# A smaller descriptor scratch for GpSimd, and seven more weight units kept in SBUF

## The chip, the cores and the metric

The kernel runs on one core of one Trainium2 chip. The metric is the device time of one execution in microseconds; a kernel's time is the median of several runs. Engines carry the names of the profile: PE (TensorE), PEld (its weight loads), DVE (VectorE), ACT (ScalarE), POOL (GpSimd), SP (SyncE).

## What is computed

The output mixes two branches of the same 2048 x 1024 input `x` by a sigmoid gate per row. Branch A is attention that runs segment by segment: 64 segments of 32 rows, each joined with 8 memory rows, and the first 8 rows of a segment's output are the next segment's memory. Branch B is a feed-forward block with 3584 hidden columns.

```python
for s in range(n_seg):                      # 64 segments, one after the other
    h = concatenate([mem, x[32*s:32*s+32]]) # 40 rows x 1024
    q, k, v = h @ Wq, h @ Wk, h @ Wv        # 32 heads of 128, each weight 1024 x 4096
    p = softmax(where(mask, q @ k.T * scale, -1e9))
    o = (p @ v) @ Wo                        # Wo: 4096 x 1024
    mem = o[:8]; outs.append(o[8:])
b = (gelu(x @ w_gate) * (x @ w_up)) @ w_down
out = g * concat(outs) + (1 - g) * b        # g = sigmoid((x * gate_w).sum(-1))
```

All tensors are bfloat16. The four weights of branch A take 32 MiB, more than the SBUF holds, and each segment needs all of them.

## The kernel before

**Order of work.** The first part, about 600 us long, is branch B in four blocks of 512 rows: `emit_H` (L449: gate and up matmuls), `down_mm` (L494), `down_out` (L510, L514: scaled copies to SBUF; L519: stores to `b_scr` in DRAM). In the same time SP copies streamed weights into one contiguous DRAM buffer, `w_scr` (`copy_wide`, L603), and POOL handles the gate values (`emit_gates`): one store of 2048 fp32 values to DRAM (L380), then 24 loads that spread them over partitions (`gload`, L385). Then come the 64 segments, strictly one after the other: memory rows of segment s are transposed and copied into `hT` at its end (L1370, L1376), and segment s+1 starts from `hT`.

**A segment.** A weight unit is 128 x 1024 (256 KiB). PE runs six projections in the order q0, k0, q1, v0, k1, v1 (`emit_P`, L958; the digit is the half of the heads), each over eight units of the contraction, and then four output groups of eight units (`emit_O`, L1121). Between them, in an order written out by hand at the end of the file, stand the transposes of q and k (`emit_T`, L1003), the scores (`emit_S`, L1038), the transposes of the probabilities (`emit_PT`, L1068) and the products with v (`emit_PV`, L1079). Each group of heads has a chain that leaves PE: scores, then DVE, ACT, DVE (L1045 to L1058, tile `pn`), `emit_PT` on PE, a DVE copy (L1073), `emit_PV` on PE, an ACT copy (L1087). Rows that a later segment takes as extra query, key and value rows are computed four segments at a time on spare matmuls (`xe`, L843, L1104) and go through DRAM: `qk_scr` (L887), `v_scr` (L860), and back as `qkst` (L715) and `vt` (L727).

**Where weights lie.** Most units stay in SBUF for all segments, in `arena`. Of each projection the units 6 and 7, and of the output groups the units 4 to 7, are streamed: `wide` lists the pairs, 19 blocks of two units (512 KiB) a segment, except that group 3 keeps its units 4 and 5. Three further units of q0 are kept in odd places. They are copied once into PSUM banks that would be idle (`KEPT`, `keep`), and put back into `vt`, `qk`, and `oT` with `rows` at the end of every segment: `back_all` (L944, L946) for unit 5, `back` (L935) for the second half of unit 4.

**The ring.** Streamed blocks go into `ring`, ten slots of one unit, so five blocks. SP issues the next load (L621) when PE has done with a block: `slot_free` counts slots, and each load waits for the matmuls that read its slots last. Loads are taken in the order of use.

**POOL's queue.** All other transfers inside the segments are issued by POOL in program order: `hT`, `xe`, `qkst`, `vt`, `bo`, the output rows (L1386) and the stores to `qk_scr` and `v_scr`. For these the descriptors lie in a scratch of SBUF, 16 KiB of each partition, that the framework sets aside at address 0.

```python
wide += [("o", o, k) for o in range(NO) for k in (4, 6) if (o, k) != (3, 4)]
...
KEPT = {("q", 0, 5, 0): [(6, 0, 0, 1024)], ("q", 0, 5, 1): [(7, 0, 0, 1024)],
        ("q", 0, 4, 1): [(3, 384, 0, 640), (5, 640, 640, 384)]}
...
emit_O(1, (1,))   # unit 4 of output group 1: a streamed block
emit_PT(2)
emit_S(3)
```

Of the kernel before, what the change touches and what calls it, by code (L numbers as in the profile page):

```python
# [5 lines left out]
BF16 = mybir.dt.bfloat16  # L6
# [122 lines left out]
def bass_gated_mix__memory_aug_recurrent_mem_tr__geglu_ffn__prompt_kernel(  # L129
# [21 lines left out]
    SEG = 32  # L151
# [16 lines left out]
    with ExitStack() as es:  # L168
# [11 lines left out]
        w_scr = nc.dram_tensor("w_scr", [19, 128, 2048], BF16)  # L180
        g_scr = nc.dram_tensor("g_scr", [S], FP32)

        def SB(shape, dt, name):
# [187 lines left out]
        def emit_gates(b):  # L371
            zs, ths = [("z", t) for t in range(4 * b, 4 * b + 4)], [("th", t) for t in range(4 * b, 4 * b + 4)]
            gv, zv = g_all[:, 4 * b:4 * b + 4], omg[:, 4 * b:4 * b + 4]
            op("act", lambda e: e.activation(gv, zv, ACTF.Tanh, scale=0.5), r=zs, w=ths)
            op("dve", lambda e: e.tensor_scalar(out=zv, in0=gv, scalar1=-0.5, scalar2=0.5,
                                                op0=ALU.mult, op1=ALU.add), r=ths, w=zs)
            op("dve", lambda e: e.tensor_scalar(out=gv, in0=gv, scalar1=0.5, scalar2=0.5,
                                                op0=ALU.mult, op1=ALU.add), r=ths, w=ths)
            if b == 3:
                op("pool", lambda e: e.dma_start(g_scr[:].rearrange("(t p) -> p t", p=128), g_all[:, :],  # L380
                                                 allow_slow_non_contiguous=True),
                   r=[("th", x) for x in range(NT)], w=[("gscr",)], dsem="gscr")

                def gload(dst, src, key):
                    op("pool", lambda e: e.dma_start(dst, src, allow_slow_non_contiguous=True),  # L385
                       r=[("gscr",), ("gz",)], w=[("gseg", key)], dsem="gseg%s" % key)

                for q in range(4):
                    gload(gseg[32 * q:32 * q + SEG, 0:NSEG - 1],
                          g_scr[EXT:EXT + (NSEG - 1) * SEG].rearrange("(s r) -> r s", r=SEG), "a%d" % q)  # L390
                    gload(gseg[32 * q:32 * q + NR, NSEG - 1:NSEG],
                          g_scr[S - SEG + EXT:S].rearrange("(s r) -> r s", s=1), "b%d" % q)
                    for u in range(GR):
                        gload(ge[32 * q + u * EXT:32 * q + (u + 1) * EXT, :],
                              g_scr[:].rearrange("(g s r) -> s r g", s=GR, r=SEG)[u, 0:EXT, :], "e%d%d" % (q, u))
# [156 lines left out]
        single = {("q", 0, 4): (half21[:, 0, :], A(21)), ("o", 3, 4): (half21[:, 1, :], A(22))}  # L552
        single[("o", 3, 5)] = (extra[:, :], A(23))

        def load_single(n):
# [4 lines left out]

        KEPT = {("q", 0, 5, 0): [(6, 0, 0, 1024)], ("q", 0, 5, 1): [(7, 0, 0, 1024)],
                ("q", 0, 4, 1): [(3, 384, 0, 640), (5, 640, 640, 384)]}
        flat_vt = vt[:, :, :].rearrange("p a b -> p (a b)")
        flat_qk = qk[:, :, :, :, :].rearrange("p a b c d -> p (a b c d)")
        flat_oT = oT[:, :, :, :].rearrange("p a b c -> p (a b c)")
        K_VT = [("vt", 0), ("vt", 1)] + [("vte", x) for x in range(2)] + [("vte", x, 0) for x in range(2)]
        K_QK = [("qk", 0), ("qk", 1), ("qke",)]
        K_OT = [("oT", 0), ("oT", 1)]
        BACK = {("q", 0, 5, 0): ([flat_vt[:, 0:512], flat_vt[:, 512:1024]], K_VT),
                ("q", 0, 5, 1): ([flat_qk[:, 0:512], flat_qk[:, 512:1024]], K_QK),  # L570
                ("q", 0, 4, 1): ([flat_oT, rows[:, :]], K_OT + [("rows",)])}

        wide = []
        for m, h in (("q", 0), ("k", 0), ("q", 1), ("v", 0), ("k", 1), ("v", 1)):
            wide += [(m, h, kc) for kc in (6, 7)]
        wide += [("o", o, k) for o in range(NO) for k in (4, 6) if (o, k) != (3, 4)]
        stream = []
        for s in range(NSEG):
            for u in wide:
                stream.append((s, u, 1 if u == ("o", 3, 5) else 2))  # L580
                if s == 0 and u == ("q", 0, 7):
                    stream += [(s, ("q", 0, 4), 1), (s, ("q", 0, 5), 2)]

        def uses(s, m, h, k):
            if m == "o":
                return 0 if k < 4 or (m, h, k) in single else (1 if (h, k) == (3, 5) else 2 * (k % 2))
            if m == "q" and h == 0 and s == 0 and k in (4, 5):
                return k - 3
            return 2 if k >= 6 else 0
# [42 lines left out]
        for b in range(4):  # L632
            mine, other = (b % 2) * 4, 4 - (b % 2) * 4
            for j in range(NJ):
# [31 lines left out]
                if b == 3 and j in (2, 6, 10, 14):  # L666
                    (load_single(("q", 0, 4)) if j == 2 else load_need(need[(4, 6, 7)[(j - 6) // 4]]))
                if b == 3 and j == 18:
                    slot_free(RING)
# [82 lines left out]
        def unit(s, m, o, k):  # L752
# [12 lines left out]
            else:  # L765
# [4 lines left out]
                if (m, h, k, j) in BACK:  # L770
                    if s > 0:
                        return BACK[(m, h, k, j)]
                    sl = slot_of[(s, (m, h, k), j if k == 5 else 0)]
                elif k >= 6:
# [27 lines left out]
        for s in range(NSEG):  # L802
# [117 lines left out]

            def back(eng, u, y):
                dst, c = BACK[u][0][y], y * 512
                if u[2] == 5:
                    pieces = [(KEPT[u][0][0], c, 0, 512)]
                elif y == 0:
                    pieces = [(3, 384, 0, 512)]
                else:
                    pieces = [(3, 896, 0, 128), (5, 640, 128, 384)]
                keys = BACK[u][1]
                if u[2] == 4:  # L930
                    keys = [("rows",)] if y else K_OT
                for bank, p0, c0, n in pieces:
                    d, sr = dst[:, c0:c0 + n], PBV[bank][:, p0:p0 + n]
                    if eng == "act":
                        op("act", lambda e, d=d, sr=sr: e.activation(d, sr, ACTF.Copy), r=[P(bank)], w=keys)  # L935
                    else:
                        op("dve", lambda e, d=d, sr=sr: e.tensor_copy(d, sr), r=[P(bank)], w=keys)

            def back_all(eng, u):
# [9 lines left out]
            def emit_P(m, h, pos, s=s):  # L949
                bank = acc(s, (m, h))  # L950
                for x in pos:
# [31 lines left out]
                    if s == 0 and (m, h) == ("q", 0):  # L983
# [3 lines left out]
                        for _ in range(1 + len(kept) % 2):  # L987
                            if kept:
                                kept.pop(0)()
                    if not (s == 0 and m == "q" and h == 0 and kc in (4, 5)):  # L990
                        slot_free(uses(s, m, h, kc))
# [365 lines left out]
            if s + 1 < NSEG:  # L1357
                op("act", lambda e, B_O=B_O: e.activation(rows[:, 0:256], PB[B_O][:, 0:256], ACTF.Copy),
                   r=[P(B_O)], w=[("rows",)])
                back("act", ("q", 0, 4, 1), 0)  # L1360
            fill(H)
# [3 lines left out]
            if s + 1 < NSEG:  # L1365
# [10 lines left out]
                op("dve", lambda e, mdst=mdst, msrc=msrc: e.tensor_copy(mdst, msrc), r=[P(B_PT)], w=[("hT",)])  # L1376
                back("act", ("q", 0, 4, 1), 1)
            flush()
            last = s == NSEG - 1
            op("dve", lambda e, s=s, B_O=B_O: e.scalar_tensor_tensor(  # L1380
                out=bo[:, :], in0=PB[B_O][:, 0:256], scalar=gseg[:, s:s + 1], in1=bo[:, :], op0=ALU.mult, op1=ALU.add),
               r=[P(B_O)] + [("gseg", "%s%d" % (k, q)) for k in "ab" for q in range(4)], w=[("bo", x) for x in range(4)])
            for put, bank in ends:
# [48 lines left out]
```

## Time and profile before

| what | value |
|---|---|
| median of 3 runs | 2458.86 us (2457.59 to 2460.99) |
| span of the profiled execution | 2450.2 us; its own time beside the span isn't listed, and the median is 8.7 us more than the span |
| instructions | 83,579 |
| read from DRAM, written | 764.52 MB, 37.22 MB |
| mean granted TensorE clock | 0.994 |

The span runs from the first to the last instruction of one execution. The page cuts it into 40 slices of about 61 us and gives the busy share of each engine in tenths. Groups of instructions are listed by line of the kernel, tile written and tile read, with the idle time of the engine before them and what ended it. "DMA ring<-w_scr" as the end of a wait means that the engine waited for the load of a streamed block.

### The profile page before, as it was taken

To read this page: it belongs to the slowest core of one execution; us is meant where nothing else is said; L and a number is where in the kernel's file an instruction comes from. 1 tells how busy PE (TensorE), PEld (TensorE's weight loads), DVE (VectorE), ACT (ScalarE), POOL (GpSimd) and SP (SyncE) were. 2 spreads that over 40 slices of the span, in tenths; PEclk is the share of its full clock that TensorE was granted. 3 is DMA by queue.
4 is the path that set the end of the run, shared out by engine and by line. 5 is a ranking of instruction groups with operands and counts; after the bars stand their busy time and mean duration, and the time that the engine had idled before them with its cause. 6 is when DMAs were issued, how large, how long until landed. Compare 5 with 4: busy or idle time off the path is not lost.

```text
span 2450.2 us, 83579 instructions
## 1 busy us (share of the span) xinstructions
PE 2198.1 (90%) x37171; PEld 1099.3 (45%) x37171; DVE 1182.3 (48%) x3451; ACT 934.6 (38%) x2212; POOL 628.7 (26%) x1122
## 2 busy tenths in 40 slices
PE   8999999999888888888888888888888888988887
PEld 4444444444444444444444444444444444444433
DVE  5626264351444444555445545444555545545444
ACT  4314132230434344444444444444444444444433
POOL 1010111200333323232323232233323232323222
PEclk9999999999999999999999999999999999999989
DMA  8726354458999999999999999999999999999998
GB/s 268 271 69 232 124 172 139 121 200 309 341 353 369 375 364 373 371 378 379 373 376 373 377 371 379 368 375 378 384 376 377 377 384 381 379 362 375 378 371 298
DMA packets 294008, 797.46 MB, mean 325 GB/s; under 512 B 48304, under 2 KB 112992, under 8 KB 292880
## 3 DMA queue, kind: packets, MB, share of 16 engines
q1 hardware_dynamic: 249380, 736.79, 80.7%
q0 software_dynamic: 43072, 54.77, 7.1%
q8 instruction: 292, 4.78, 0.8%
q10 hardware_dynamic: 1196, 0.56, 0.1%
q14 instruction: 68, 0.56, 0.1%
HBM read 764.52 MB, written 37.22 MB: 327 GB/s over the span
## 4 chain that ended last, share of the span: by engine, by line
PE 55%; DMA 30%; DVE 7%; ACT 5%; issue 2%; POOL 0%; SPq 0%; DVEq 0%
DMA ring<-w_scr 29%; PE pba L958 6%; PE pbb L958 6%; PE pbc L843 5%; PE pba L1121 3%; PE pbb L1121 3%; PE pbe L1068 2%; PE pbh L449 2%; PE pbg L449 2%; PE pbf L449 2%; PE pbe L449 2%; PE pba L449 2%; PE pbb L449 2%; PE pbc L449 2%; PE pbd L449 2%
## 5 line engine op out<-in xcount | busy, mean ns | idle before, releaser
L958 PE MATMUL pba<-arena,hT 128*32 128x512 bf16 x4416 | 357.1, 381 | 2.5 <-issue 2.3
L958 PE MATMUL pbb<-arena,hT 128*32 128x512 bf16 x4416 | 350.5, 382 | 1.5 <-issue 1.5
L1051 ACT ACTIVATE pbd<-pbd 104x160 f32<-104x160 f32 x256 | 71.9, 281 | 550.1 <-DVE pbd L1049 550.1
L727 POOL DMA_DIRECT2D vt<-v_scr x252 | 147.5, 589 | 395.3 <-PE pbf L1079 272.2
L1011 DVE COPY qk<-pbe 128x512 bf16<-128x512 bf16 x129 | 89.2, 692 | 317.4 <-PE pbe L1003 317.4
L1073 DVE COPY ptb<-pbe 80x320 bf16<-80x320 bf16 x256 | 82.1, 321 | 273.2 <-PE pbe L1068 273.2
L843 PE MATMUL pbc<-arena,xe 128*32 128x512 bf16 x2208 | 184.0, 380 | 1.3 <-issue 0.7
L1386 POOL DMA_DIRECT2D out_dram<-bo x252 | 125.5, 505 | 214.0 <-DVE bo L1380 205.1
L958 PE MATMUL pbb<-ring,hT 128*32 128x512 bf16 x1536 | 152.5, 386 | 30.9 <-DMA ring<-w_scr 28.4
L958 PE MATMUL pba<-ring,hT 128*32 128x512 bf16 x1542 | 153.2, 385 | 28.6 <-DMA ring<-w_scr 26.3
L958 PEld LDWEIGHTS pba<-arena,hT 128*32 128x32 bf16 x4416 | 115.9, 97 | 98.7 <-issue 6.6
L958 PEld LDWEIGHTS pbb<-arena,hT 128*32 128x32 bf16 x4416 | 115.9, 97 | 86.5 <-issue 6.1
L1058 DVE TENSOR_TENSOR pn<-pbd,rr 104x256 bf16<-104x256 f32 (+1 forms) x512 | 141.9, 318 | 8.7
L964 ACT ACTIVATE rows<-pba 128x512 bf16<-128x512 f32 x128 | 76.4, 597 | 156.0 <-PE pba L958 156.0
L887 POOL DMA_DIRECT2D qk_scr<-rowsx x60 | 47.4, 790 | 327.4 <-DVE rowsx L884 327.4
L1052 DVE TENSOR_REDUCE rs<-pbd 104x4 f32<-104x160 f32 x256 | 83.0, 324 | 88.9 <-ACT pbd L1051 88.9
L1087 ACT ACTIVATE oT<-pbf 128x256 bf16<-128x256 f32 x256 | 97.5, 381 | 74.1 <-PE pbf L1079 73.3
L1121 PE MATMUL pba<-ring,oT 128*32 128x256 bf16 x1792 | 108.6, 278 | 17.1 <-DMA ring<-w_scr 16.4
L1121 PE MATMUL pba<-arena,oT 128*32 128x256 bf16 x2176 | 119.4, 280 | 3.6 <-ACT oT L1087 1.8
L1068 PE MATMUL pbe<-ident,pn 104*80 104x104 bf16 x1024 | 95.1, 216 | 30.4 <-ACT qk L1009 12.7
L1121 PE MATMUL pbb<-arena,oT 128*32 128x256 bf16 x2176 | 119.8, 275 | 2.8 <-ACT oT L1087 0.4
L1121 PE MATMUL pbb<-ring,oT 128*32 128x256 bf16 x1792 | 109.2, 275 | 12.9 <-DMA ring<-w_scr 10.9
(260 smaller groups left out, 4298.9 us busy)
## 6 DMA issues: line engine op xcount, KB each, us to landing
ring<-w_scr SPq DMA_DIRECT2D x1216, 512.0 KB, 6.3
arena<-in_B_w_gate_dram SPq DMA_DIRECT2D x27, 1024.0 KB, 5.2
arena<-in_B_w_up_dram SPq DMA_DIRECT2D x27, 1024.0 KB, 7.4
qkst<-qk_scr POOLq DMA_DIRECT2D x126, 64.0 KB, 5.6
qk_scr<-rowsx POOLq DMA_DIRECT2D x60, 128.0 KB, 5.7
arena<-in_B_w_down_dram SPq DMA_DIRECT2D x7, 1024.0 KB, 11.3
arena<-in_A_Wk_dram SPq DMA_DIRECT2D x6, 1024.0 KB, 6.6
arena<-in_A_Wv_dram SPq DMA_DIRECT2D x6, 1024.0 KB, 9.5
```

Of the source, the lines that this page charges most:

```text
L449: ins = e.matmul(PB[bank][:, :], lhsT=wv[:, kc, col:col + 128], rhs=xb[:, kc, :], start=(kc == 0), stop=(kc == KC - 1))
L727: op("pool", lambda e: e.dma_start(vt[2 * SEG:KEYS, par, :], v_scr[s // GR, h, 2 * par:2 * par + 2, s % GR, :, :]), r=[("vscr", s // GR, h ...
L843: ins = e.matmul(PB[B_X][32 * gq:32 * gq + 32, :], lhsT=xe[:, us[-1], :], rhs=us[gq // 2][0][gq % 2], start=(n == 0), stop=(n == KC - 1), ...
L958: ins = e.matmul(PB[bank][32 * gq:32 * gq + 32, :], lhsT=hT[:, kc, :], rhs=us[gq // 2][0][gq % 2], start=(x == 0), stop=(x == KC - 1), ski ...
L1011: op("dve", lambda e: e.tensor_copy(qk[:, m, :, 0:SEG, :], src), r=[P(B_T)], w=[("qk", m)])
L1052: op("dve", lambda e: e.tensor_reduce(rsv, sv, AX.X, ALU.add), r=[P(B_S)], w=[("rs",)])
L1058: op("dve", lambda e, c0=c0, k0=k0, n=n: e.tensor_tensor(out=pn[0:104, :, c0:c0 + 2 * n].rearrange("p i (two c) -> p i two c", two=2), in0 ...
L1068: ins = e.transpose(PBV[B_PT][0:KEYS, 512 + i * 128:512 + i * 128 + 104], pn[0:104, i, :], ident[0:104, 0:104])
L1073: op("dve", lambda e: e.tensor_copy(ptb[0:KEYS, :, :, :], src), r=[P(B_PT)], w=[("ptb",)] + first)
L1087: op("act", lambda e: e.activation(dst, src[:, :, :, 0:SEG], ACTF.Copy), r=[P(B_PV)], w=[("oT", o % 2)])
L1121: ins = e.matmul(PB[B_O][32 * q:32 * q + 32, 0:256], lhsT=oT[:, o % 2, k, :], rhs=u[q // 2][:, (q % 2) * 256:(q % 2 + 1) * 256], start=(o ...
L1386: op("sp" if last else "pool", lambda e, d=d, b=b: e.dma_start(d, b), r=[("bo", x)], w=[("out", s, x)], dsem="%s%d" % ("end" if last else ...
```

## The change

POOL's scratch is cut from 16 KiB to 2 KiB of a partition, and the freed 14 KiB hold a new tensor `low` of seven units. It takes the units 6 and 7 of the output groups 0, 1 and 2, and the second half of unit 4 of q0 (called `("q", 1, 4)`). The three output blocks leave `wide`, so 16 blocks a segment are streamed, and the copies into `w_scr` fall from 19 to 16. The unit of q0 is no longer put away in PSUM and put back, and segment 0 doesn't stream it. Four loads on SP fill `low` in the third block of branch B. The gate's store is cut in two transfers of 1024 values, and each load of 63 x 32 values in two, of 32 x 32 and 31 x 32.

```diff
+        LOW = 2048
+        nc.dynamic_dma_scratch_size = LOW
+        for held_set in nc.m.functions[0].allocations:
+            if held_set.name == "DynamicDMAScratchLoc_set":
+                held_set.tensor_shape = [128, LOW]
...
+        low = nc.alloc_sbuf_tensor_at("low", [128, 7 * 1024], BF16, offset=LOW)
...
-                op("pool", lambda e: e.dma_start(g_scr[:].rearrange("(t p) -> p t", p=128), g_all[:, :],
...
+                for z in range(0, NT, 8):
+                    op("pool", lambda e, z=z: e.dma_start(g_scr[z * 128:(z + 8) * 128].rearrange("(t p) -> p t", p=128),
+                                                          g_all[:, z:z + 8], allow_slow_non_contiguous=True),
...
+                    for z, n in ((0, SEG), (SEG, NSEG - 1 - SEG)):
+                        gload(gseg[32 * q:32 * q + SEG, z:z + n],
...
+        LOWS = [("o", 0, 6), ("o", 1, 6), ("o", 2, 6), ("q", 1, 4)]
+        for i, (m, o, k) in enumerate(LOWS):
+            for y in range(2 if m == "o" else 1):
+                single[(m, o, k + y)] = (low[:, (2 * i + y) * 1024:(2 * i + y + 1) * 1024], ("L", i))
...
-        KEPT = {("q", 0, 5, 0): [(6, 0, 0, 1024)], ("q", 0, 5, 1): [(7, 0, 0, 1024)],
-                ("q", 0, 4, 1): [(3, 384, 0, 640), (5, 640, 640, 384)]}
+        KEPT = {("q", 0, 5, 0): [(6, 0, 0, 1024)], ("q", 0, 5, 1): [(7, 0, 0, 1024)]}
...
-        wide += [("o", o, k) for o in range(NO) for k in (4, 6) if (o, k) != (3, 4)]
+        wide += [("o", o, k) for o in range(NO) for k in (4, 6) if ("o", o, k) not in single]
...
-                    stream += [(s, ("q", 0, 4), 1), (s, ("q", 0, 5), 2)]
+                    stream += [(s, ("q", 0, 5), 2)]
...
+                if b == 2 and j in (19, 21, 23, 25):
+                    load_low((j - 19) // 2)
...
-                back("act", ("q", 0, 4, 1), 0)
...
-                back("act", ("q", 0, 4, 1), 1)
```

The order of the matmuls, and all that is written out by hand at the end of the file, stays as it was.

## Prediction

> **What bounds the kernel now.** I read the page from the top: busy shares, slices, the chain that ended last, transfers.
>
> ```profile
> span 2450.2 us, 83579 instructions
> PE 2198.1 (90%) x37171; PEld 1099.3 (45%) x37171; DVE 1182.3 (48%) x3451; ACT 934.6 (38%) x2212; POOL 628.7 (26%) x1122
> ...
> PE   8999999999888888888888888888888888988887
> ...
> DMA  8726354458999999999999999999999999999998
> ...
> PE 55%; DMA 30%; DVE 7%; ACT 5%; issue 2%; POOL 0%; SPq 0%; DVEq 0%
> ...
> ring<-w_scr SPq DMA_DIRECT2D x1216, 512.0 KB, 6.3
> ```
>
> From the tenth slice on, where the segments are, the transfers are busy at nine tenths or more and PE drops to eight tenths. The chain alternates between PE and DMA. 1216 loads are 19 a segment. The stretches give the size of both, and the rows of the memory copy (L1376) give the segments: 63 copies, the first at 642.9 us and the last at 2413.8, so 62 segments of 1770.9 / 62 = 28.56 us.
>
> ```profile
> 600.00:642.90 42.90, 36.53 (x754) 19.57 (x742) 19.36 (x65) 14.24 (x33) 16.15 (x29) 0.95 0.98 353
> 642.90:2413.80 1770.90, 1545.41 (x33072) 795.34 (x33072) 871.57 (x2936) 738.19 (x1779) 530.77 (x938) 0.99 1.00 373
> ```
>
> ```profile
> L1376 DVE COPY hT<-pbe x63: 190/192/193, 642.9 to 2413.8; 128x64 bf16<-128x64 bf16 x63
> ```
>
> Transfers: a DMA share of 1.00 at 373 GB/s, which is 373 x 28.56 = 10.65 MB a segment. PE: 1545.4 / 62 = 24.93 us busy, 3.64 us idle a segment. So the transfers have no time to spare, and PE little. What PE's idle time waits for decides what fewer bytes are worth (waits of the segments, PE and then its weight loads; columns: us in total, times, longest):
>
> ```profile
> PE pbb L958 <- DMA ring<-w_scr: 27.7, 64, 1.3
> PE pba L958 <- DMA ring<-w_scr: 24.6, 45, 2.1
> PE pbe L1370 <- ACT rows L1358: 22.9, 47, 0.5
> PE pbf L1079 <- issue: 22.2, 49, 0.5
> PE pba L1121 <- DMA ring<-w_scr: 14.7, 25, 1.4
> PE pbe L1068 <- ACT qk L1009: 12.4, 46, 0.4
> PE pbb L1121 <- DMA ring<-w_scr: 10.9, 25, 1.0
> PE pbe L1068 <- DVE pn L1058: 8.8, 23, 0.7
> ```
>
> ```profile
> PEld pbe L1003 <- ACT rows L964: 36.3, 72, 0.8
> PEld pbd L1038 <- DVE qk L1024: 32.0, 58, 0.9
> PEld pbe L1068 <- DVE pn L1058: 31.3, 89, 0.9
> ```
>
> The ring costs PE 27.7 + 24.6 + 14.7 + 10.9 = 77.9 us, 1.26 us a segment. Most of the rest are hand-overs to ACT and DVE that fewer bytes don't shorten. The second fence warns: in most of the 62 segments PE's next weights also stand waiting for a chain through ACT or DVE.
>
> **The change part by part.**
>
> *Three blocks fewer.* 3 x 524,288 bytes = 1.57 MB leave the segment: 10.65 - 1.57 = 9.08 MB, at 373 GB/s 24.3 us instead of 28.56. That is below PE's 24.93 us busy time plus its other waits, 3.64 - 1.26 = 2.38 us, together 27.3 us. The transfers stop being the bound, and PE with its chains is next. Do the ring's waits then end? All three blocks come out of the output groups, while the projections still take 12 blocks in the first two thirds of a segment. A load may start when the block five places ahead of it is done. With 28.56 / 19 = 1.5 us a block now that leaves some 7.5 us, and the load takes
>
> ```profile
> DMA to landing us min/median/max: 4.0/6.3/8.7
> ```
>
> (loads of the ring in the segments). The median is that of a saturated queue. With 16 blocks, 27.5 / 16 x 5 = 8.6 us stand on average against a landing that moves towards 4.0. Where the projections take blocks faster, the five in the ring ahead of q0 help. I leave 4 us of the 77.9 as waits that stay; the ends are 0 and half of L958's, 26 us.
>
> *What is late next.* A ring wait that stands inside a chain costs nothing today, since PE would have waited for the chain at its end. One segment shows it, PE first and then DVE:
>
> ```profile
> 1015.68 0.29 PE L1121 MATMUL pbb<-ring,oT 128*32 128x256 bf16 x4 [0.17 <-DMA ring<-w_scr]
> 1016.07 0.33 PE L1068 MATMUL pbe<-ident,pn 104*80 104x104 bf16 x3
> ```
>
> ```profile
> 1015.26 0.17 DVE L1054 TENSOR_TENSOR rr<-mx,bm 104x8 f32<-104x8 f32 x1
> 1015.46 0.55 DVE L1058 TENSOR_TENSOR pn<-pbd,rr 104x256 bf16<-104x256 f32 x2
> ```
>
> PE waits 0.17 us for the block of group 1 and starts the third `emit_PT` at 1016.07, 0.06 us after `pn` is done at 1015.46 + 0.55 = 1016.01. Without the ring wait it would start at the same time. This place (unit 4 of group 1, just ahead of `emit_PT(2)`) is where most of L1121's 25.6 us can stand, since the other two waits of the output groups come while the ring is refilled between groups. I take 18 of the 25.6 us as given back. Of L958's 52.3 us, those ahead of `emit_T(0)`, of `emit_S(0)` and of the second `emit_PT` fall before chains that are at their limit in 72, 58 and 46 cases. Those behind them (k0, v0, k1) are free. I take a third, 17 us, as given back. Both ends stay for the range: nothing given back, or all of it.
>
> *`back` goes.* Three ACT copies a segment fall away:
>
> ```profile
> L935 ACT ACTIVATE oT<-pbd x63: 591/591/592, 642.3 to 2413.3; 128x512 bf16<-128x512 bf16 x63
> L935 ACT ACTIVATE rows<-pbd x63: 277/278/278, 642.9 to 2413.8; 128x128 bf16<-128x128 bf16 x63
> L935 ACT ACTIVATE rows<-pbf x63: 491/491/493, 643.2 to 2414.1; 128x384 bf16<-128x384 bf16 x63
> ```
>
> 1.36 us of ACT a segment, but they stand behind the copy of the memory rows (L1358), and ACT then waits for the end of q0. Value 0. They can't have cost more than the wait for the tile they delay; nothing is listed as waiting for L935.
>
> *Start.* `keep` loses one of three units, segment 0 streams 1.75 MB less (three blocks and one unit), and `low` is loaded earlier, in the third block of branch B. Cover there: a DMA share of 0.3 to 0.5 (slices 5 to 7); without cover 1.75 MB / 373 GB/s = 4.7 us. The gain lies between 0 and PE's idle time of 42.9 - 36.5 = 6.4 us in the stretch from 600 us. Between ends so close I take 2 us.
>
> *The scratch.* It is an eighth. The diff cuts transfers of 2048 and 2016 rows and leaves those of 512 (L887), so I take the room to be 1024 to 2048 rows. In the segments POOL issues (transfers, KB each, us to landing):
>
> ```profile
> qkst<-qk_scr POOLq DMA_DIRECT2D x126, 64.0 KB, 5.6
> qk_scr<-rowsx POOLq DMA_DIRECT2D x60, 128.0 KB, 5.7
> hT<-xT_scr POOLq DMA_DIRECT2D x64, 64.0 KB, 5.4
> bo<-b_scr POOLq DMA_DIRECT2D x63, 64.0 KB, 5.3
> out_dram<-bo POOLq DMA_DIRECT2D x252, 16.0 KB, 5.3
> vt<-v_scr POOLq DMA_DIRECT2D x252, 16.0 KB, 5.4
> ```
>
> In rows: 126 x 128 + 60 x 512 + 64 x 128 + 63 x 128 + 252 x 32 + 252 x 16 = 75,136, or 1174 a segment, so one turn of the room takes 25 to 50 us. A transfer has landed after 5.7. POOL finds old room free, and I value this at 0 in the segments. In the gate part rows come faster:
>
> ```profile
> 419.87 16.12 POOL L385 DMA_DIRECT2D gseg<-g_scr  x24 [9.72 <-DMA g_scr<-ptb]
> 435.98 5.58 POOL L519 DMA_DIRECT2D b_scr<-ring  x10
> 454.82 5.57 POOL L519 DMA_DIRECT2D b_scr<-ring  x10 [13.26 <-ACT ring L510]
> ```
>
> 24 loads carry 4 x (2016 + 24 + 4 x 128) = 10,208 rows, several turns. If each turn waits for a landing, POOL ends up to some 12 us later, but it is idle for 13.3 us before the next stores. Value 0; without that cover 12 us, once.
>
> **Sum.** 77.9 - 4 - 18 - 17 + 2 = 41 us off the span, 2450.2 - 41 = 2409. The median of the runs stands 8.7 us above the span, which gives 2458.9 - 41 = **2418 us**.
>
> **The rivals.**
>
> *Nothing is given back.* For it: the scores that start a chain are PE's own work, so a chain also starts earlier by all that was saved ahead of it. Against it: the wait at 1015.68 stands between the scores and the transpose, and the 0.06 us leave no slack there. All 77.9 and the 2 us go: 2379.
>
> *The chains take it all.* For it: the 72, 58 and 89 cases above. Against it: 52.3 us stand before L958, and most projections feed no chain at their limit. About 2457.
>
> *POOL runs out of room* (slower). The tightest transfer is `vt` of the second half: issued after the first `emit_PV`, read by the third.
>
> ```profile
> 1011.13 0.32 PE L1079 MATMUL pbf<-ptb,vt 80*128 80x80 bf16 x4
> 1017.41 0.32 PE L1079 MATMUL pbf<-ptb,vt 80*128 80x80 bf16 x4
> ```
>
> From the end at 1011.45 to 1017.41 are 5.96 us, and the landing takes 5.4, so 0.5 us are spare. If POOL must first wait for a landing of its own (5.3), PE stands 4.8 us. One such wait in every fourth segment, the period of the `qk_scr` stores, is 15 x 4.8 = 72 us: 2490. From nine cases on (9 x 4.8 = 43) the gain is gone. Against it: the turn of 25 us or more. By the Trainium skill, "DMA: Bandwidth & Descriptors", section "SWDGE vs HWDGE vs iDMA", the scratch holds rings of 16-byte descriptors; 2048 / 16 = 128 for each of 16 engines, 2048 rows, is an estimate from that page, which no row here shows yet. By it the room is at the upper end of what I took from the diff, and this rival weaker.
>
> **How the numbers follow.** Forecast 0.64, nothing given back 0.14, all taken 0.08, out of room or another late POOL transfer 0.14. The forecast's own ends, with half of L958's waits staying or with nothing left out but the given-back time, are 2395 and 2440. The range reaches from the first rival to just short of no gain: 2372 to 2454. A measurement of this kernel can tell about 0.2%, 5 us. Faster by more than that: 0.64 + 0.14 + 0.02 of the third case = 0.80; within it 0.06; slower 0.14.
>
> **What would show it.** Right: 1024 loads of the ring from `w_scr`, a DMA share near 0.9, ring waits of PE below 10 us, more waits of L1068 for `pn` and of L1038 for `qk`, no L935, a segment near 27.9 us. Wrong: the share stays at 1.00 with ring waits at L958; PE waits for `vt` at L1079; POOL's transfers last longer than their 0.5 to 0.8 us; branch B ends later than 600 us.

## The result, and the profile after

The changed kernel takes **2419.49 us** (median of 4 runs, 2415.72 to 2426.18); the kernel before, run beside it, 2459.93 us (4 runs). The ratio is 0.9838, 95% interval [0.9801, 0.9875], so 40 us less. The forecast was 2418 us. The profiled execution took 2426.18 us, 1.9 us more than its span. It is the longest of its four, and before's span of 2450.2 with the same 1.9 us would be 2452, below its four runs here. So the pair of profiles differs by 26 us where the medians differ by 40; the other 14 us are scatter of single executions: before's profiled one is some 7 us shorter than its median, after's 7 us longer.

The page of the changed kernel, the lines that answer to those of before:

```profile
span 2424.3 us, 83116 instructions
PE 2166.2 (89%) x37099; PEld 1109.6 (46%) x37155; DVE 1182.4 (49%) x3450; ACT 860.6 (35%) x2023; POOL 632.8 (26%) x1127
...
DMA  8726346267989999899998999999999989999986
...
HBM read 663.85 MB, written 35.64 MB: 289 GB/s over the span
...
PE 63%; DMA 14%; DVE 11%; ACT 7%; issue 4%; POOL 1%; SPq 0%; DVEq 0%; ACTq 0%; POOLq 0%
...
ring<-w_scr SPq DMA_DIRECT2D x1024, 512.0 KB, 6.1
```

1024 loads, 16 a segment, and 101 MB less read. In the chain that ended last, DMA falls from 30% to 14% and does not vanish. The segments, by the copy of the memory rows and by the stretches (columns as in the prediction):

```profile
L1381 DVE COPY hT<-pbe x63: 191/192/193, 649.5 to 2386.5; 128x64 bf16<-128x64 bf16 x63
```

```profile
649.50:2386.50 1737.00, 1514.23 (x33072) 804.81 (x33072) 872.12 (x2936) 665.15 (x1593) 531.84 (x938) 0.99 0.92 325
```

62 segments take 1737.0 us, 28.02 each instead of 28.56: 33.9 us less. The first copy comes 6.6 us later (649.5 against 642.9), and what follows the last one is 1.4 us longer: -33.9 + 6.6 + 1.4 = -25.9, the difference of the spans. The transfers run at 325 GB/s with a share of 0.92, and yet PE still waits for them. The share is a mean over stages: from the first to the last streamed block of the projections, 15.9 us of a segment, the trace shows 288 GB/s at a share of 0.87 in the first third, then 363 at 0.99 and 380 at 1.00, and from the first streamed block of the output groups to the segment's end 287 GB/s at 0.84. PE's waits in the segments (us in total, times, longest):

```profile
PE pbe L1074 <- DVE pn L1064: 35.0, 61, 0.7
...
PE pbb L964 <- DMA ring<-w_scr: 19.9, 34, 1.7
PE pba L964 <- DMA ring<-w_scr: 18.9, 31, 2.1
...
PE pbf L1085 <- DMA vt<-v_scr: 1.7, 4, 0.5
PE pbb L1127 <- DMA ring<-w_scr: 1.0, 2, 0.6
...
PE pba L1127 <- DMA ring<-w_scr: 0.2, 1, 0.2
```

Two things are to be seen. The ring's waits at the output groups are gone (25.6 us to 1.2), but at the projections 38.8 of 52.3 us stay. And `emit_PT` now waits for `pn` 61 times in 62 segments (before: 23), 35.0 us against 8.8; 59 of these waits (before: 22) are at the third `emit_PT`.

PE's idle time in the segments is 1737.0 - 1514.2 = 222.8 us; before it was 225.5. So nearly the whole gain in the segments lies in PE's *busy* time, 1545.4 to 1514.2 us for the same 33,072 matmuls. The segments' stretch limited to the matmuls of the projections (first fence before, L958; second after, L964) shows where:

```profile
642.90:2413.80 1770.90, 818.16 (x11904) 276.45 (x11904) 0.99 1.00 373
```

```profile
649.50:2386.50 1737.00, 796.39 (x11904) 284.08 (x11904) 0.99 0.92 325
```

The same 11,904 matmuls are busy for 21.8 us less at the same clock; the 7,936 of the output groups go from 330.3 (L1121) to 314.5 us (L1127). What changed in these lines is how often the weights of a matmul come late. PEld's waits for the ring, before and after:

```profile
PEld pbb L958 <- DMA ring<-w_scr: 82.5, 153, 1.8
PEld pba L958 <- DMA ring<-w_scr: 79.9, 150, 2.6
...
PEld pbb L1121 <- DMA ring<-w_scr: 29.5, 56, 1.3
PEld pba L1121 <- DMA ring<-w_scr: 25.9, 47, 1.8
```

```profile
PEld pba L964 <- DMA ring<-w_scr: 42.9, 65, 2.3
PEld pbb L964 <- DMA ring<-w_scr: 42.0, 67, 1.8
...
PEld pbb L1127 <- DMA ring<-w_scr: 2.5, 5, 0.8
PEld pba L1127 <- DMA ring<-w_scr: 0.4, 1, 0.4
```

Before, the weight loads waited 217.8 us in 406 places while PE showed 77.9 us of idle time for the ring; after, it is 87.8 us in 138 places beside 40.0. So for most of the time in which a weight load waits for the ring PE is not idle in this profile, in which the ends of matmuls are modelled.

Ahead of the segments something new appears. POOL in the last block of branch B (start, busy time, engine, line; in brackets the idle time before and what ended it):

```profile
401.74 0.92 POOL L391 DMA_DIRECT2D g_scr<-ptb  x1 [0.24 <-issue]
416.52 0.89 POOL L391 DMA_DIRECT2D g_scr<-ptb  x1 [13.86 <-issue]
426.43 0.80 POOL L396 DMA_DIRECT2D gseg<-g_scr  x1 [9.02 <-DMA g_scr<-ptb]
429.65 4.63 POOL L396 DMA_DIRECT2D gseg<-g_scr  x7 [2.42 <-issue]
436.69 4.61 POOL L396 DMA_DIRECT2D gseg<-g_scr  x7 [2.41 <-issue]
445.30 4.62 POOL L396 DMA_DIRECT2D gseg<-g_scr  x7 [4.00 <-issue]
452.43 3.76 POOL L396 DMA_DIRECT2D gseg<-g_scr  x6 [2.52 <-issue]
456.18 8.51 POOL L531 DMA_DIRECT2D b_scr<-ring  x15
```

The second half of the gate's store starts 13.9 us after the first was issued. Some 4 us of that are not the scratch's: the gate values of this half are ready only at 406.75 (DVE, L387). The loads pause four more times, 11.4 us together. Each of these five held transfers starts 0.3 to 0.4 us after the landing of one that POOL had issued before it: the first half of the store landed at 416.10, and the first load, issued at 426.43, at 429.35. The stores to `b_scr`, of which before the first ten began at 435.98, now begin at 456.18. ACT waits for the buffers of these stores, DVE for ACT, and PE for DVE. ACT and then PE, and the 10.2 us in which the granted clock was halved:

```profile
460.51 0.69 ACT L522 ACTIVATE ring<-pba,ptb 128x512 bf16<-128x512 f32 x1 [31.87 <-DMA b_scr<-ring]
```

```profile
456.53 1.89 PE L461 MATMUL pbh<-arena 128*128 128x512 bf16 x8
467.40 3.59 PE L461 MATMUL pbe<-arena 128*128 128x512 bf16 x8 [8.97 <-DVE arena L476]
```

```profile
462.40:472.60 10.20, 5.20 (x13) 1.90 (x14) 5.47 (x8) 3.73 (x7) 5.08 (x10) 0.50 0.27 54
```

PE stands 9.0 us, where before it had no gap. The granted clock falls to 0.50 at 462.4, 4.0 us into the gap, and stays there for 10.2 us, 5.2 of them with PE at work again.

By the Trainium skill, "DMA: Bandwidth & Descriptors", section "SWDGE vs HWDGE vs iDMA", the prediction had worked out an estimate of 2048 rows of room. The trace does not bear it out: the first load (32 x 32 rows of 4 bytes) and the second (31 x 32) are 2016 rows together, and the second is held for 2.42 us, until the first has landed.

### The profile page after: what moved, and what is told of

It is laid out like the page before. It is cut to its first block, busy times and chain, and to the rows that moved or that the text cites. A ratio compares the mean times of both kernels' runs of the same rounds, so it can differ in the third digit from the quotient of the medians.

```text
span 2424.3 us, 83116 instructions
## 1 busy us (share of the span) xinstructions
PE 2166.2 (89%) x37099; PEld 1109.6 (46%) x37155; DVE 1182.4 (49%) x3450; ACT 860.6 (35%) x2023; POOL 632.8 (26%) x1127
## 4 chain that ended last, share of the span: by engine, by line
PE 63%; DMA 14%; DVE 11%; ACT 7%; issue 4%; POOL 1%; SPq 0%; DVEq 0%; ACTq 0%; POOLq 0%
DMA ring<-w_scr 13%; PE pbb L964 9%; PE pba L964 8%; PE pbc L867 6%; PE pba L1127 4%; PE pbb L1127 3%; PE pbe L1074 3%; PE pbc L1110 2%; PE pba L461 2%; PE pbe L461 2%; PE pbf L461 2%; PE pbb L461 2%; PE pbg L461 2%; PE pbd L461 2%; PE pbh L461 2%
## 5 line engine op out<-in xcount | busy, mean ns | idle before, releaser
L964 PE MATMUL pba<-arena,hT 128*32 128x512 bf16 x4416 | 354.5, 382 | 0.3 <-issue 0.3
L964 PE MATMUL pbb<-arena,hT 128*32 128x512 bf16 x4416 | 350.3, 383 | 0.0
L964 PE MATMUL pbb<-ring,hT 128*32 128x512 bf16 x1536 | 151.4, 385 | 23.0 <-DMA ring<-w_scr 22.1
L964 PE MATMUL pba<-ring,hT 128*32 128x512 bf16 x1540 | 151.6, 383 | 20.1 <-DMA ring<-w_scr 19.3
L964 PEld LDWEIGHTS pba<-arena,hT 128*32 128x32 bf16 x4416 | 115.5, 97 | 102.8 <-ACT rows L970 6.7
L964 PEld LDWEIGHTS pbb<-arena,hT 128*32 128x32 bf16 x4416 | 115.8, 97 | 90.7 <-issue 3.8
L1074 PEld LDWEIGHTS pbe<-ident,pn 104*80 104x80 bf16 x1024 | 62.5, 116 | 138.8 <-DVE pn L1064 69.6
L970 ACT ACTIVATE rows<-pbb 128x512 bf16<-128x512 f32 x128 | 76.3, 596 | 133.8 <-PE pbb L964 133.8
L1127 PE MATMUL pbb<-arena,oT 128*32 128x256 bf16 x2176 | 121.3, 279 | 2.2
L1009 PE MATMUL pbe<-ident,rows 128*32 128x128 bf16 x4096 | 103.8, 221 | 18.8 <-ACT rows L970 8.9
```

The lines of the kernel that those rows point to most:

```text
L964: ins = e.matmul(PB[bank][32 * gq:32 * gq + 32, :], lhsT=hT[:, kc, :], rhs=us[gq // 2][0][gq % 2], start=(x == 0), stop=(x == KC - 1), ski ...
L970: op("act", lambda e: e.activation(rows[:, :], PB[bank][:, :], ACTF.Copy), r=[P(bank)], w=[("rows",)])
L1009: ins = e.transpose(PBV[B_T][j:j + 32, i * 128:(i + 1) * 128], rows[:, i * 128 + j:i * 128 + j + 32], ident[:, :])
L1074: ins = e.transpose(PBV[B_PT][0:KEYS, 512 + i * 128:512 + i * 128 + 104], pn[0:104, i, :], ident[0:104, 0:104])
L1127: ins = e.matmul(PB[B_O][32 * q:32 * q + 32, 0:256], lhsT=oT[:, o % 2, k, :], rhs=u[q // 2][:, (q % 2) * 256:(q % 2 + 1) * 256], start=(o ...
```

## The experiments

Each time stands beside runs of the kernel before on the same chip. Ratios are to those, with 95% intervals.

### The small scratch alone

Before with the 2 KiB scratch and the two cuts of the gate transfers; nothing kept, 19 blocks streamed.

```diff
+        nc.dynamic_dma_scratch_size = LOW
-                op("pool", lambda e: e.dma_start(g_scr[:].rearrange("(t p) -> p t", p=128), g_all[:, :],
+                for z in range(0, NT, 8):
...
+                    for z, n in ((0, SEG), (SEG, NSEG - 1 - SEG)):
```

> The kernel before with the scratch of 2 KiB and the gate transfers cut in two, and nothing else: 19 blocks streamed, freed SBUF unused. Theory: the small scratch costs only in the gate part, where POOL ended some 20 us later in the changed kernel and the segments began 6.6 us later; so 5 to 10 us more than before (2465 to 2470), the segments at 28.5 us as before, ring waits of L958 and L1121 as before. Rival (room runs out in the segments too): segments over 28.8 us, PE waits for vt at the products with v, 2480 or more. Rival (the scratch costs nothing, the late start is scatter): 2460 within 5.

Measured: 2469.46 us (12 runs) against 2459.53 (23 runs), ratio 1.0042 [1.0018, 1.0065]: 10 us slower, as the theory had it.

```profile
L1387 DVE COPY hT<-pbe x63: 191/192/193, 651.9 to 2423.4; 128x64 bf16<-128x64 bf16 x63
```

The segments take (2423.4 - 651.9) / 62 = 28.57 us, as before; the first copy comes 9.0 us later. PE between 380 and 520 us, before and with the small scratch:

```profile
380.00:520.00 140.00, 140.00 (x663) 63.88 (x661) 61.96 (x92) 37.93 (x74) 29.53 (x47) 1.00 0.48 149
```

```profile
380.00:520.00 140.00, 132.87 (x601) 60.11 (x612) 57.10 (x84) 34.09 (x68) 32.33 (x52) 0.98 0.47 125
```

PE's gap is 6.5 us here. So the scratch costs about 10 us once, in the gate part, and nothing in a segment that these runs can tell.

### The kept half of q0's unit 4 alone

After with only that half unit in `low` (no copies back at the end of a segment), and all 19 blocks streamed again.

```diff
-        LOWS = [("o", 0, 6), ("o", 1, 6), ("o", 2, 6), ("q", 1, 4)]
+        LOWS = [("q", 1, 4)]
```

> The changed kernel with only the q0 unit kept in the freed SBUF; the three output blocks are streamed again, 19 a segment, and the gate part is the changed kernel's. Against the kernel that only cuts the scratch (2469.5 us): theory (the three ACT copies stand behind the path): 2469 within 6, segments at 28.5 us. Rival (the copies hold up the start of the next segment): at least 10 us less and segments below 28.4 us.

Measured: 2474.57 us (9 runs), ratio 1.0055 [1.003, 1.0081]. The segment is (2431.1 - 650.5) / 62 = 28.72 us:

```profile
L1381 DVE COPY hT<-pbe x63: 191/192/193, 650.5 to 2431.1; 128x64 bf16<-128x64 bf16 x63
```

Against the small scratch alone, measured on another chip, the ratios overlap (1.0042 and 1.0055). The time lies in the theory's range; the segment is 0.15 us longer than there, where the rival asked for a shorter one. So the three ACT copies a segment were worth nothing, and no gain of the change comes from them. PE's busy time in the segments is 1546.0 us, so they do not explain its fall in after either.

### Is a hidden wait really free?

Before, with the second and third unit of output group 1 exchanged, so that the wait for the streamed unit 4 moves behind the third `emit_PT`.

```diff
-        OORD = ((1, 4, 3, 0, 5, 2, 6, 7), (2, 4, 1, 5, 3, 6, 0, 7), (0, 4, 1, 5, 2, 3, 6, 7), (0, 4, 1, 5, 3, 2, 6, 7))
+        OORD = ((1, 4, 3, 0, 5, 2, 6, 7), (2, 1, 4, 5, 3, 6, 0, 7), (0, 4, 1, 5, 2, 3, 6, 7), (0, 4, 1, 5, 3, 2, 6, 7))
```

> The kernel before with two units of output group 1 exchanged: the streamed unit 4 behind the third transpose of the probabilities and the kept unit 1 ahead of it. No transfer is added or taken away. Theory (the ring wait at this place is hidden in the chain): ring waits of the output groups fall from 25.6 us to 10 or less, waits of the transposes for pn grow from 8.8 us to 20 or more, and the time stays at 2460 within 6. Rival (the ring wait costs its own length): about 19 us less, 2441.

Measured: 2458.45 us (12 runs), ratio 0.9995 [0.9974, 1.0016].

```profile
PE pbe L1068 <- DVE pn L1058: 30.2, 57, 0.7
PE pbb L958 <- DMA ring<-w_scr: 29.2, 63, 1.8
...
PE pba L958 <- DMA ring<-w_scr: 18.0, 39, 1.3
...
PE pba L1121 <- DMA ring<-w_scr: 8.6, 20, 1.0
```

The wait for `pn` rises from 8.8 to 30.2 us, those of `pba` and `pbb` at L1121 fall from 14.7 and 10.9 to 8.6 and 5.5, and the time is the same. The 14.1 us that stay at the output groups are more than the theory's 10; the waits for `pn` and the time came as it said. The ring's wait at this place stood inside a chain that would have made PE wait anyway: what is saved there is given back to `pn`.

### Which blocks to keep

After keeps blocks of the output groups. Here the same room holds three projection blocks from the middle of a segment instead.

```diff
-        LOWS = [("o", 0, 6), ("o", 1, 6), ("o", 2, 6), ("q", 1, 4)]
+        LOWS = [("q", 1, 7), ("v", 0, 7), ("k", 1, 7), ("q", 1, 4)]
```

> The changed kernel with another choice of what stays: unit 7 of q1, v0 and k1 (both halves) instead of units 6 and 7 of the output groups 0 to 2; again 16 blocks streamed. Theory (stage): in the changed kernel the transfers are still the bound in the projections, which take 12 blocks in some 16 us, so the 39 us of ring waits at the projections fall below 15 us; waits of the output groups come back to at most 20 us but stand inside the chain of the probabilities; time 2400 to 2410. Rival (each load simply takes 6 us and five fit in the ring, whichever they are): ring waits at the projections stay at 30 us or more, time 2419 within 5 or above.

Measured: 2434.63 us (6 runs), ratio 0.99 [0.9869, 0.9931], segment 28.06 us. The theory failed and its rival held:

```profile
PE pbb L967 <- DMA ring<-w_scr: 21.4, 47, 1.5
...
PE pba L967 <- DMA ring<-w_scr: 13.8, 20, 1.6
```

35.2 us of ring waits stay at the projections. They only moved: in after they stand at unit 7 of q1 (0.18 us a segment), unit 7 of v0 (0.18) and in k1 and v1; here at unit 7 of q0 (0.19) and in k0 (0.34), behind the output groups, whose seven blocks are used within 8.6 us. Where the blocks still follow each other closely, PE still waits.

### A deeper ring, all 19 blocks streamed

Before with the small scratch and the freed room as ring: 16 slots, eight blocks instead of five. No block is kept, so a segment moves as many bytes as before. The gate transfers are issued later (next experiment).

```diff
-    RING = 10
+    RING = 16
...
+        ring_low = low[:, 0:6 * 1024].rearrange("p (a b) -> p a b", a=6)
+        def rslots(a, n):
+            return ring[:, a:a + n, :] if a < 10 else ring_low[:, a - 10:a - 10 + n, :]
```

> The freed SBUF as ring instead of kept units: 16 slots, eight blocks, all 19 blocks streamed as before, gate transfers late. Theory (the transfers run at their rate, 373 GB/s over the segments, so more blocks in flight bring nothing): segments at 28.3 to 28.6 us, a DMA share of 1.00, time 2452 to 2460. Rival (a load takes 6 us whatever the traffic, and five blocks in flight are too few): ring waits of L958 and L1121 together fall from 78 us below 30, time 2415 to 2430.

Measured: **2392.92 us** (5 runs), ratio 0.9721 [0.9697, 0.9745]. The theory that the rate bounds the kernel falls by 60 us, and the rival's 2415 to 2430 is beaten too. Stretch, landing (of the loads into the ten old slots) and waits of the segments; `low` holds the six new slots:

```profile
647.80:2361.60 1713.80, 1501.80 (x33072) 814.40 (x33072) 872.18 (x2936) 739.91 (x1779) 533.70 (x938) 0.99 1.01 385
```

```profile
DMA to landing us min/median/max: 3.8/7.1/10.7
```

```profile
PE pba L1141 <- DMA ring<-w_scr: 0.5, 1, 0.5
PE pbb L1141 <- DMA low<-w_scr: 0.5, 1, 0.5
...
PE pba L978 <- DMA ring<-w_scr: 0.4, 1, 0.4
PE pbb L978 <- DMA low<-w_scr: 0.2, 1, 0.2
```

The same bytes a segment now move at 385 GB/s instead of 373, the segment takes 27.64 us, and 77.9 us of ring waits have become 1.6. The share was 1.00 before and is 1.01 here: it does not tell a rate that is reached from a queue that always has something in it. Each single load takes longer (a median of 7.1 us against 6.3), and PE still waits less.

### Gate transfers later

After, with the gate's stores and loads moved on POOL from the head of the last block of branch B to behind the `b_scr` stores that held PE up.

```diff
-            if b == 3:
-                for z in range(0, NT, 8):
+        def gates_out():
+            for z in range(0, NT, 8):
...
+                if b == 3 and j == 1:
+                    gates_out()
```

> The changed kernel with the gate stores and loads moved on POOL behind the stores of the third block of branch B, where POOL is idle for over 100 us. Theory: the late start goes away, the memory copy of segment 0 comes at 641 to 645 us instead of 649.5, and the time falls by 5 to 9 us to about 2412. Rival (the late start is scatter, or has another cause): 2419 within 4.

> After with the late gate transfers, unedited from the earlier run, now beside the others on one chip. Theory: 5 to 10 us less than after's 2419 to 2428, so 2412 to 2421 us, segment 28.1 us. Rival (a gap of PE only moves to the next late load): the same as after within its scatter, 2420 to 2428 us.

Measured on two chips: 2421.19 us (6 runs), ratio 0.9846 [0.9818, 0.9873], and 2420.00 us (6 runs), ratio 0.9838 [0.9808, 0.9868]. The first theory's 2412 us did not come, and the second run's rival held: no gain over after that these runs can tell. The first copy comes at 639.4 us in the first run, earlier than the theory's 641 to 645, but at 647.8 in the second; the segments take 28.11 and 28.03 us. The gap of 9 us is gone, but one of 2.8 us (first run) or 4.5 us (second) stands a little later:

```profile
486.72 3.59 PE L462 MATMUL pbf<-arena 128*128 128x512 bf16 x8 [4.46 <-DMA arena<-in_B_w_up_dram]
```

PE now waits for a weight of branch B while the gate's 4-byte rows are on their way; that these delay the load was not tried by itself.

### After once more, unedited

> The changed kernel, unedited, for comparison on one chip with the others of this group and with the kernel with late gate transfers (2421.2 us). If the late gate transfers are worth the 10 us by which they moved the start of the segments (649.5 to 639.6 us), this takes 2428 to 2432; if the start is bought back later or the first runs on another chip compare as they stand, 2419 to 2422.

Measured: 2427.56 us (6 runs, 2423.05 to 2440.39) against 2460.25 (14 runs), ratio 0.9865 [0.9839, 0.989]; segment 28.03 us, first copy at 652.4, PE's gap 9.1 us. So the change is worth 33 to 40 us, and two medians of after, of 4 and 6 runs on two occasions, differ by 8 us while those of before beside them differ by 0.3.

### Kept blocks spread over the segment

Three blocks kept as in after, but apart from each other: one of q1, one of v1, one of output group 1. First with the late gate transfers, then without, then the first once more beside the second.

```diff
-        LOWS = [("o", 0, 6), ("o", 1, 6), ("o", 2, 6), ("q", 1, 4)]
+        LOWS = [("q", 1, 7), ("v", 1, 7), ("o", 1, 6), ("q", 1, 4)]
```

> The changed kernel with late gate transfers and with what stays spread over the segment: unit 7 of q1 and of v1 (both halves) and units 6 and 7 of output group 1. 16 blocks streamed. In the changed kernel the streamed loads run at 206 GB/s in the first 3 us of a segment, some 345 in the middle and 201 in the last 4; with the kept blocks in q1, v0 and k1 the waits moved to q0 and k0 (35 us). Theory (waits come from the densest stretch of streamed blocks): ring waits at the projections fall below 20 us, segments below 27.9 us, time 2405 to 2415. Rival (what is left of ring waits is hidden by the chains anyway): the waits fall, but the time stays within 5 us of the kernel with late gate transfers (2421).

> After with other blocks kept (q1 and v1 units 6 and 7, o1 units 6 and 7), the gate transfers where after has them. Two edits made the version of 2387 us; this one has only the placement. Theory (placement carries nearly all of it): the segments are 27.45 us as there, the start has the PE gap of 9 us near 458 us again, and the time is 2390 to 2398 us. Rival (the late gate transfers carried a good part): above 2400 us.

> The best version, unedited, beside the others on one chip: 2380 to 2392 us, so 30 us or more under gates_late_2 on the same chip if the placement is what gains. If the first run was a fast chip, the difference is below 25 us.

Measured: 2387.28 us (4 runs), ratio 0.9691 [0.9666, 0.9717], 18 us below the theory's range; without the late gate transfers 2386.73 us (5 runs), 0.9699 [0.9667, 0.9731]; the first again 2383.55 us (6 runs), 0.9682 [0.9648, 0.9716]. On that last chip after's blocks with late gate transfers took 2420.00, so placement alone is worth 36 us, and the late gate transfers again nothing that these runs can tell. (PE's gap in the gate part was 5.6 us without them, not the 9 us expected.) Without the late gate transfers:

```profile
646.90:2349.20 1702.30, 1498.08 (x33072) 803.65 (x33072) 872.09 (x2936) 664.45 (x1593) 531.83 (x938) 1.00 0.94 331
```

```profile
PE pbe L1080 <- DVE pn L1070: 32.4, 62, 0.7
...
PE pbb L970 <- DMA ring<-w_scr: 8.5, 14, 1.4
...
PE pba L970 <- DMA ring<-w_scr: 4.2, 11, 0.8
```

Same bytes, same depth as after, a segment of 27.46 us, and 13.3 us of ring waits (0.6 of them at the output groups) instead of 40.0. By their medians these are the fastest versions here.

### Half and half

One block kept (q1), and four units of the room as ring: seven blocks deep, 18 a segment streamed, late gate transfers.

```diff
-    RING = 10
+    RING = 14
...
-        LOWS = [("o", 0, 6), ("o", 1, 6), ("o", 2, 6), ("q", 1, 4)]
+        LOWS = [("q", 1, 7), ("q", 1, 4)]
```

> Late gate transfers; of the freed room two units hold the block of q1, one the half of q0's unit 4, and four are ring: seven blocks in the ring, 18 a segment streamed. Theory (what counts is that no load is late; depth does it as well as placement): ring waits of PE below 5 us in the segments and the segment at 27.45 to 27.65 us, 2385 to 2395 us. Rival (bytes still count, and 18 blocks stay near the transfers' rate): a DMA share of 1.00 and a segment over 27.7 us, above 2396 us.

Measured: 2393.69 us (6 runs), ratio 0.9735 [0.9697, 0.9773].

```profile
648.20:2359.50 1711.30, 1497.81 (x33072) 815.40 (x33072) 872.11 (x2937) 666.23 (x1593) 533.71 (x938) 1.00 0.99 367
```

27.60 us a segment, and no wait for the ring is listed. The time lies inside the theory's range. The rival's share of 0.99 is there too, but not its 27.7 us. With the ring's waits near zero the two deep rings stay 0.14 to 0.18 us a segment behind the spread blocks' 27.46. PE's waits for other transfers are one candidate (`vt` 5.6 us with the ring of 16 slots); it was not tried.

### What the experiments say together

A streamed block is in time if the block five places ahead (eight in the deep ring) is finished early enough, and that is a matter of place, not of the mean. For each block of after, means of 62 segments, worked out from its trace: the lead, from the start of the block five ahead to the start of the block itself; the landing time of its load; what is left between landing and use; and PE's idle time for the load there.

```
block     lead us   landing us   left us   idle us a segment
q0 unit 6   12.6       6.7         5.4        0.000
q0 unit 7   10.7       5.9         4.1        0.000
k0 unit 6   10.7       5.0         3.8        0.000
k0 unit 7    8.4       4.3         3.3        0.000
q1 unit 6    7.1       4.2         2.5        0.017
q1 unit 7    6.3       4.9         0.9        0.178
v0 unit 6    8.0       6.0         1.5        0.000
v0 unit 7    7.8       6.6         0.6        0.176
k1 unit 6    8.1       6.9         0.7        0.088
k1 unit 7    7.6       6.4         0.7        0.041
v1 unit 6    7.9       6.8         0.6        0.052
v1 unit 7    7.0       6.1         0.4        0.073
o0 unit 4    8.4       6.5         1.4        0.009
o1 unit 4    7.8       6.4         0.9        0.010
o2 unit 4    9.9       6.2         3.2        0.000
o3 unit 6   11.8       6.4         4.8        0.000
```

Over all loads of the segments:

```profile
DMA to landing us min/median/max: 3.3/6.1/9.5
```

The blocks with less than 1 us left hold 0.62 of the 0.65 us a segment. The lead alone does not decide: the landing time changes with the place too, from 4.2 us at unit 6 of q1 to 6.9 at unit 6 of k1. In the spread blocks the shortest leads, 6.9 and 6.3 us in k0, come with landings of 4.9 and 5.2 and almost no wait, and every other block has 1.1 us or more left.

The mean lead is 5 x 28.02 / 16 = 8.8 us in after and 5 x 27.46 / 16 = 8.6 in the spread blocks, so it does not tell the two apart. The change put the surplus into the output groups, whose waits were hidden, and into q0 and k0, whose blocks are loaded meanwhile: their 16 us of waits ended. From q1 to v1 the waits stayed, 36 us before and 39 after. With eight blocks the mean lead is 8 x 27.64 / 19 = 11.6 us, more than the longest landing of 10.9.

One reading stays open. The 12 blocks of the projections are used within 15.9 us in after, which is 397 GB/s for them alone, more than the 385 GB/s of the deep ring's segments. So in that stretch the rate of the transfers may bind as well as the lead; no run separates the two there, and more depth and an even spacing ease both.

## Why the prediction was right, and where its working was not

The time was met (2418 forecast, 2419.49 measured), and the mechanism in outline: the output groups' waits end, and about as much as forecast is given back to the chains. That the number came within 2 us is in part luck, twice over. First, two errors of the sum nearly cancel within the segments:

| term | forecast | measured (profiles before and after) |
|---|---|---|
| ring waits of PE that end | -77.9 + 4 = -73.9 | -77.9 + 40.0 = -37.9 |
| given back to other waits of PE | +18 + 17 = +35 | +35.2 (idle time -2.7 in all, less the -37.9) |
| PE's busy time | 0 | -31.2 |
| sum | -38.9 | -33.9 |
| start of the segments | -2 | +6.6 |
| behind the last segment | 0 | +1.4 |

Second, the span was forecast at 2409 and came out at 2424.3, 15 us more. The prediction added 8.7 us from span to median as if they belonged to the kernel; an execution takes 1.9 us more than its span, and the rest was that before's profiled execution was a short one. After's was a long one, and that made up for the 15 us. The measured column rests on one execution of each kernel and carries this scatter; beside the 2427.56 us of after once more, the forecast is 10 us low.

- **"I leave 4 us of the 77.9 as waits that stay."** This step failed: 40.0 us stay, beyond its upper end of 26. It set a mean lead of 8.6 us against "a landing that moves towards 4.0". The shortest landing is 3.3, but the median is 6.1, and from v0 to v1 the means are 6.0 to 6.9 us at leads of 7.0 to 8.1. "The five in the ring ahead of q0 help" was right for q0 and k0, and no further. The prediction saw that "the projections still take 12 blocks in the first two thirds" and did not put a number to it. The spread blocks, with as many bytes and the same ring, show what it was worth.
- **"The ring costs PE 77.9 us."** Mis-sized: that is only the idle time. The weight loads waited 217.8 us, and PE's busy time falls with them, by 31.2 us in after, by 43.6 with the deep ring (1545.4 to 1501.8) and by 47.3 with the spread blocks. The deep ring streams all 19 blocks, so it is not the bytes; it keeps the ACT copies too. That late weights stretch the busy time follows from this correlation; it was not isolated.
- **"So the transfers have no time to spare."** Wrong as a statement on the mean rate. The deep ring moves the same blocks at 385 GB/s and gains 67 us. Taken over a segment, what was short was the lead of a ring of five blocks. That the transfers stop being the bound with 16 blocks was right by half: the share is 0.92, and blocks still come late.
- **Given back.** Right in kind; the sum of 35 is closer than its parts. The exchange in output group 1 shows that the wait at unit 4 was hidden; 17.5 of the 25.6 us did stand there in before's trace, as the 18 had it. The wait for `pn` grew by 26.2 us, though, and the other 9 us, against 17 for L958, are the balance of the rest, in which three waits for ACT and DVE grew by 4 to 6.5 us each: L1044 for `qk` (4.0 to 8.0), L1009 for `rows` (3.7 to 8.6), L895 for `rowsx` (4.0 to 10.5). PE also reached the chains earlier by its shorter busy time, which the sum did not have.
- **`back`: 0.** Right; the kept half unit alone brings nothing.
- **The scratch.** In the segments 0: right, with 1.7 us of waits for `vt` in four places (before 1.3 in one), so the third rival (POOL out of room) did not come there. "Value 0; without that cover 12 us, once" in the gate part: the value failed. That a transfer waits for a landing was right, and so was the cover of 13.3 us, but POOL's delay was mis-sized. Counted from the last gate values (408.67 before, 406.75 after), the stores to `b_scr` begin 22.1 us later, not 12. Of these the two halves of the store, now one after the other, take 8.1 and the pauses of the loads 11.4. Without the cover's 13.3 us 8.8 are left, and PE's gap is 9.0. That the small scratch alone costs 10 us, near the 12, is chance.
- **Start: -2.** Not seen; the first copy comes 6.6 us later because of the scratch.
- **Slips in its figures, of no weight.** The rows of POOL's transfers add up to 75,200, 1175 a segment. The three blocks and one unit are 1.84 MB. The lower end of 2395 follows from none of the terms: with no wait staying they give 2414. And 72 waits in 62 segments cannot all stand ahead of `emit_T(0)`.

Of the signs named ahead, the 1024 loads, the share near 0.9, the waits for `pn` and the segment near 27.9 us (28.02) came. "Ring waits of PE below 10 us" did not, and it was the one that spoke of the failed step. Of the signs against it, "branch B ends later than 600 us" came: its last stores to `b_scr` start at 608.8 us, before at 599.0. The rival in which nothing is given back (2379) is refuted by the exchange in group 1; the one in which the chains take all (2457) by the result.

## What to carry to other kernels

A DMA share of 1.00 with waits for loads doesn't say that bytes bound the kernel: compare, place by place, the time from a buffer's release to its use with the landing time there, and try either depth or an even spacing before cutting bytes. A wait is worth what stands behind it: find which waits lie inside a chain that ends later anyway, and value these at nothing. Where weights come late, PE's idle time may be only a part of their cost; look at the weight loads' waits and at the busy time of the same matmuls too.

## What the runs showed of the hardware that was not expected

- With 2 KiB of scratch POOL held a second transfer of 1024 rows, and loads of about 1000 rows for 2.4 to 4.0 us, until an earlier transfer had landed; each then started 0.3 to 0.4 us after that landing. The profile puts these pauses down to "issue", not to a wait. With 16 KiB all 24 loads had gone out in 16.1 us without one.
- On this one core the transfers kept up 385 GB/s over 1714 us, with 512 KiB loads, where five blocks in place of eight had given 373 GB/s at a share that already showed 1.00.
- In a gap of 9.0 us on PE the granted clock fell to 0.50 after 4.0 us and stayed there for 10.2 us.
